# Clustered attention and two mixture layers on one core: direct transfers of the maxima's row, new places, and another form of the tail

## The chip, the cores and the metric

One Trainium2 chip, one of its cores. The metric is the device time of one launch in microseconds (us).

## The reference

Three layers in a row, all in float32:

```python
# attention: q, k, v of shape (4, 8, 768, 64), 16 centroids for each head
q_assign = argmax(normalised(q) @ normalised(c).T); k_assign = the same of k
scores = where(q_assign == k_assign, q @ k.T / 8, -1e9)
x = softmax(scores) @ v                       # to (3072, 512)
# first mixture layer: w_in (512, 2048), w_out (2048, 512)
h = x @ w_in; y = (h * cos(h)) @ w_out
# soft mixture: phi (512, 32), 8 experts of 4 slots, w1 (8, 512, 1024), w2 (8, 1024, 512)
logits = y @ phi
d = softmax over tokens; c = softmax over the 32 slots
slot_input = d.T @ y
slot_out[e] = relu(slot_input[e] @ w1[e]) @ w2[e]
out = c @ slot_out                            # (3072, 512)
```

## The kernel before, in words

**Attention.** The 32 heads are worked on in 16 pairs. Each pair has 12 units `u` (two halves of the queries, six blocks of 128 keys), and each unit has two scores, one for each head. `score` (L394) makes two matmuls, one with 97 rows (L399) and one with 128 (L400), from a stack tile `st` in SBUF that holds the split q and k, the cluster codes and, in partition 96, the negated row maxima. ScalarE takes the exponent (L403), `av` (L405) multiplies with `v` on TensorE two units later, and GpSimd adds up the denominators (L417, L420). The maxima come from `smax` (L354): 24 small score matmuls a pair (L364), each followed by a VectorE reduction (L366). They rotate through three PSUM banks. `smax_fin` (L368) merges 12 of them, and `smax_row` (L376) transposes the result on TensorE (L379), lets VectorE write `mrow` (L381), and defers two transfers: `mrow` to a DRAM tile `mds`, and `mds` to partition 96 of `st`.

Everything around the scores is put at numbered places by hand: a pair has 48 of them, four for each unit, and `POS` (L521) holds the places of the steps for a pair in the steady state, `FIRST` (L533) those for the first two pairs. For pair j, the preparation (`place_p`, L560: transposes "T", clusters "c", "m", code rows "rows", loading of the next pair "ld") runs two pairs ahead and the maxima ("sm", "fin") one pair ahead. The last "sm" of the first half of the queries and its "fin" have to be through by place 48, where the pair's first score stands. The conversion of the weights from 64-bit words ("cv", `conv_do` L455, eight steps, mostly VectorE's) handles two blocks a pair; its input comes through `conv_load` (L448) into one buffer, `w64`, and the weights' products with phi stand at "wp". "vm" has the places of the mean of v (`prep_vm`, GpSimd; `prep_vm2`, TensorE) and of `sumq` (L427), the sums of the denominators.

All transfers are issued by SP, in the order of the program. `defer(n, ...)` (L162) puts a transfer off by n places, and `tick` (L165), called at each place, issues what is due. A transfer that has to wait for its data holds up all that follow it on SP.

**First mixture layer.** 96 chunks `c` (token tile and quarter of the hidden width; the last two tiles are taken together). `hchunk` (L131) makes 12 matmuls, `post1`, `post2` the cosine, `gtr`, `gev`, `logit` the transposed product with the weights and phi, and `soft1` to `soft5` a running softmax of the group of tokens that is done. `xload` (L94) fetches a tile's numerators `xn` and reciprocals `rc`. In the last chunks the freed buffers take the experts' weights: 16 pieces of 2 MB (`load_piece`, `load_part`, `load_halves`, L740 to L754).

**Tail.** From L989 on: the last softmax, `apz`, `acct`, `si`, `sit` (the slots' input), `expert_in` (pieces 0 to 7), `expert_tr`, `expert_out` (L1140, pieces 8 to 15, 32 output columns of the array for each of four experts, so four column positions), and then for each half of the output width `regroup` (L1151) and twelve calls of `final` (L1161), which multiply the combination weights with the slots' output and write it out. Between them the combination weights `ck` are split into a high and a low part, twice each (`ct_dve`, L904), transposed to `ctk` (`ct_pe`, L910: 24 transposes in four groups) and evicted by ScalarE (`ct_ev`, L918). `final` then needs one fp32r matmul over 128 rows per token tile (L1168), evicted by ScalarE (L1172) or VectorE (L1174).

Of the kernel before, what the change touches and what calls it, by code (L numbers as in the profile page):

```python
# [19 lines left out]
P = 128  # L20
# [6 lines left out]
def clustered_attention_then_soft_moe(  # L27
# [60 lines left out]
    mds = {(i, c): dram.tile([6, P], F32, name=f"mds{i}_{c}") for i in range(NPAIR) for c in range(2)}  # L88
# [5 lines left out]
    def xload(t):  # L94
        b, tt = divmod(t, KT)
        c = slice(tt * P, (tt + 1) * P)
        mx = R["mx"]
        xn = mx.tile([P, DT, P], F32, tag="xn", name=f"xn{t}", bufs=1)
        rc = mx.tile([P, DT, P], F32, tag="rc", name=f"rc{t}", bufs=1)
# [50 lines left out]
    with ExitStack() as a:  # L150
# [225 lines left out]
        def smax_row(i, qc):  # L376
# [141 lines left out]
        def at4(g, q, f, *args):  # L518
# [14 lines left out]
        FIRST = {  # L533
            "eqt": 7,
            "mask": 8,
            "rows": [9, 12, 12, 10],
            "cv": [3, 6, 8, 11, 15],
            "ld": 9,
            "wp": [21, 26, 36],
            "sm0": [2, 2, 5, 5, 6, 7, 8, 12, 15],  # L540
            "sm1": [13, 15, 16, 21, 22, 24, 24, 25, 26, 26, 28, 29, 17, 29, 31, 33, 34, 38, 40, 41, 42, 42, 44, 45],
            "fin0": [15, 19],
            "fin1": [33, 35],
        }

        def place_conv(n, g):
# [3 lines left out]
            if n + 1 < len(conv):  # L550
                at(g + pos[5] // 4 + 1, 0, conv_load, n + 1)
# [69 lines left out]
        def m_open():  # L621
            pp_stack.close()
            R["mx"] = mx_stack.enter_context(tc.tile_pool(name="mx", bufs=2, side="right"))
# [124 lines left out]

    def load_halves(n, w):
        for e in range(2):  # L750
            load_part(n, 2 + e, w[:, e])
# [4 lines left out]
    with ExitStack() as m:  # L756
# [299 lines left out]
        for h in range(2):  # L1056
# [6 lines left out]
            if h == 0:  # L1063
                ct_pe(1)
# [159 lines left out]
```

## Time and profile before

| what | value |
|---|---|
| time, median of 3 runs | 959.75 us (957.63 to 960.16) |
| time of the profiled execution | 960.29 us |
| its span, first to last instruction | 958.4 us |
| mean granted TensorE clock | 0.989 |
| TensorE busy | 904.9 us, 94% |
| VectorE busy | 716.2 us, 75% |
| ScalarE busy | 674.5 us, 70% |
| GpSimd busy | 459.3 us, 48% |
| attention, first to last score | about 32 to 503 us |
| first mixture layer | about 504 to 890 us |
| tail | about 890 to 958 us |

PE is TensorE's matmuls, PEld its weight loads, DVE VectorE, ACT ScalarE, POOL GpSimd, SP the queue that issues the transfers. A wait names the engine and line that sat idle, then what ended it. In a windows row the granted clock (1.00 is 2.4 GHz), the DMA engines' busy share and the GB/s that they moved stand at the end. A matmul's end is modelled, so a matmul may count as busy while it waits to drain. An fp32 matmul shows as two instructions.

### The profile page before, as it was taken

What the parts mean: (1) busy time and instruction counts of PE and PEld (TensorE: products, weight loads), DVE (VectorE), ACT (ScalarE), POOL (GpSimd) and SP (SyncE); (2) the same over time, 40 slices, a digit from 0 to 9 for tenths busy, and PEclk for the clock granted to TensorE, in tenths of its full rate; (3) what the DMA queues carried; (4) which work ended last, traced back from release to release, by engine and by line L of the source; (5) the groups of instructions that cost most, each with busy time, mean ns of one, the idle gap of its engine ahead of it and who ended that gap; (6) DMA issues with size and microseconds to landing.
All of it is one profiled execution on the core that took longest, in us unless ns stands there. A gap on an engine that the chain in (4) does not pass through costs nothing.

```text
span 958.4 us, 16925 instructions
## 1 busy us (share of the span) xinstructions
PE 904.9 (94%) x5994; PEld 622.8 (65%) x5994; DVE 716.2 (75%) x1459; ACT 674.5 (70%) x1420; POOL 459.3 (48%) x342
## 2 busy tenths in 40 slices
PE   5798999999999999999999999999999999999995
PEld 3465666666666666656656777777777777677543
DVE  6778888988888888879786777777777777775402
ACT  4657888777887778867664677767776777676423
POOL 3437877788777878776862222222222222220000
PEclk9889999999999999999999999999999999999998
DMA  8966667776668766676231043304331111117899
GB/s 173 211 149 157 162 175 196 192 197 155 166 176 213 191 172 166 174 186 166 89 95 54 24 132 117 125 25 132 119 123 36 33 37 31 45 26 295 333 360 326
DMA packets 132515, 142.18 MB, mean 148 GB/s; under 512 B 58408, under 2 KB 105808, under 8 KB 132432
## 3 DMA queue, kind: packets, MB, share of 16 engines
q1 hardware_dynamic: 132432, 141.11, 53.2%
q8 instruction: 47, 0.77, 0.3%
q14 instruction: 36, 0.29, 0.1%
HBM read 86.27 MB, written 17.06 MB: 108 GB/s over the span
## 4 chain that ended last, share of the span: by engine, by line
PE 68%; DVE 11%; ACT 9%; DMA 7%; issue 2%; SPq 2%; POOL 0%; ACTq 0%; POOLq 0%
PE h L138 21%; PE o L412 12%; PE sm L364 6%; PE s L399 6%; PE s L400 5%; PE gt L784 3%; DVE mc L366 3%; DMA mds<-mrow 3%; PE lp L810 2%; PE accp L893 2%; DVE qlo L275 2%; ACT L772 2%; DMA st<-mds 2%; PE he L1101 1%; ACT L848 1%
## 5 line engine op out<-in xcount | busy, mean ns | idle before, releaser
L138 PE MATMUL h<-wc,xhi 128*128 128x512 f32 x768 | 249.6, 406 | 6.7 <-DVE gg L777 6.5
L420 POOL TENSOR_TENSOR ps<-ps,a 128x768 f32<-128x768 f32 x120 | 235.3, 1961 | 37.9 <-ACT a L403 18.2
L366 DVE TENSOR_REDUCE mc<-sm 128x1 f32<-128x384 f32 x384 | 199.1, 547 | 30.3 <-PE sm L364 27.9
L403 ACT ACTIVATE a<-s 128x384 f32<-128x384 f32 x384 | 175.8, 491 | 26.2 <-PE s L400 20.4
L138 PEld LDWEIGHTS h<-wc,xhi 128*128 128x128 f32 x768 | 137.3, 189 | 56.9 <-DVE kk L147 15.9
L138 PE MATMUL h<-wc,xlo 128*128 128x512 f32 x384 | 151.7, 395 | 0.0
L399 PE MATMUL s<-st 97*128 97x384 f32 x384 | 141.8, 369 | 7.3 <-DMA st<-mds 6.9
L412 PE MATMUL o<-a,vt 128*64 128x384 f32 x768 | 147.7, 506 | 0.0
L364 PE MATMUL sm<-st 96*128 96x384 f32 x384 | 135.8, 385 | 10.1 <-DVE mc L366 6.1
L400 PE MATMUL s<-st 128*128 128x384 f32 x384 | 130.5, 340 | 0.0
L364 PEld LDWEIGHTS sm<-st 96*128 96x128 f32 x384 | 72.4, 194 | 50.4 <-DVE mc L366 17.5
L777 DVE SCALAR_TENSOR_TENSOR gg<-kk,h 128x512 f32<-128x512 f32 x96 | 66.0, 687 | 50.6 <-ACT kk L774 47.8
L772 ACT ACTIVATE kk<-kk 128x512 f32<-128x512 f32 x96 | 60.6, 631 | 42.0 <-DVE kk L147 41.7
L399 PEld LDWEIGHTS s<-st 97*128 97x128 f32 x384 | 73.1, 190 | 23.1 <-issue 11.1
L412 PEld LDWEIGHTS o<-a,vt 128*64 128x64 f32 x768 | 47.2, 137 | 57.6 <-issue 57.3
L109 POOL TENSOR_TENSOR xn<-xn,rc 128x512 f32<-128x512 f32 x24 | 31.3, 1304 | 109.0 <-DMA rc<-recs 109.0
L138 PEld LDWEIGHTS h<-wc,xlo 128*128 128x128 f32 x384 | 72.2, 188 | 17.0
L400 PEld LDWEIGHTS s<-st 128*128 128x128 f32 x384 | 73.4, 191 | 0.0
L417 POOL TENSOR_TENSOR ps<-a,a 128x768 f32<-128x768 f32 x30 | 54.8, 1827 | 37.5 <-ACT a L403 33.7
L113 POOL TENSOR_TENSOR xn<-xn,rc 128x512 f32<-128x512 f32 x24 | 32.0, 1332 | 84.0 <-DVE rc L111 78.9
L121 POOL TENSOR_TENSOR xlo<-xn,xhi 128x512 fp32r<-128x512 f32 x24 | 36.5, 1522 | 67.5 <-DVE xhi L120 66.0
L147 DVE SCALAR_TENSOR_TENSOR kk<-kk,h 128x512 f32<-128x512 f32 x96 | 66.0, 688 | 3.3
(218 smaller groups left out, 1530.0 us busy)
## 6 DMA issues: line engine op xcount, KB each, us to landing
w<-in_moe_w_dram SPq DMA_DIRECT2D x8, 2048.0 KB
wh<-in_moe_w_dram SPq DMA_DIRECT2D x26, 512.0 KB
st<-qhi SPq DMA_DIRECT2D x32, 384.0 KB
st<-khi SPq DMA_DIRECT2D x64, 192.0 KB
w<-in_moe_w_out_dram SPq DMA_DIRECT2D x16, 512.0 KB
w<-in_moe_w_in_dram SPq DMA_DIRECT2D x16, 512.0 KB
qt<-in_q_dram SPq DMA_DIRECT2D x32, 192.0 KB
kt<-in_k_dram SPq DMA_DIRECT2D x32, 192.0 KB
```

Source lines behind the costliest of these rows:

```text
L138: PE.matmul(h, lhsT=x[:, d, :], rhs=wc[f][:, w, d, :], start=(n == 0), stop=(n == 3 * DT - 1))
L147: DVE.scalar_tensor_tensor(out=a, in0=a, scalar=-TWO_PI, in1=h, op0=ALU.mult, op1=ALU.add)
L364: PE.matmul(m[:, 0:QW], lhsT=st[0:96, Q1 + h, qt * P:(qt + 1) * P], rhs=st[0:96, K1 + h, half * QW:(half + 1) * QW], start=True, stop=True)
L366: DVE.tensor_reduce(out=s["mc"][:, col:col + 1], in_=m[:, 0:QW], op=ALU.max, axis=AX.X)
L399: PE.matmul(x[:, 0:QW], lhsT=st[0:97, K1 + h, ks], rhs=st[0:97, Q1 + h, qs], start=True, stop=False)
L400: PE.matmul(x[:, 0:QW], lhsT=st[:, K2 + h, ks], rhs=st[:, Q2 + h, qs], start=False, stop=True)
L403: ACT.activation(out=T[i][u][:, h, :], in_=x[:, 0:QW], func=AF.Exp, scale=scale)
L412: PE.matmul(s["o"][64 * h:64 * h + 64, 0:QW], lhsT=s["v"][:, h, kt, :], rhs=t[:, h, :], start=(kt == 0), stop=(kt == KT - 1))
L417: (DVE if i == NPAIR - 1 else POOL).tensor_tensor(out=ps, in0=s[u - 1], in1=t, op=ALU.add)
L420: (DVE if i == NPAIR - 1 else POOL).tensor_tensor(out=ps, in0=ps, in1=t, op=ALU.add)
L772: ACT.activation(out=r, in_=r, func=AF.Sin, scale=0.5)
L777: DVE.scalar_tensor_tensor(out=R["g", t][:, f * 512:(f + 1) * 512], in0=r, scalar=0.5, in1=h, op0=ALU.subtract, op1=ALU.mult)
```

## The change

1. `smax_row` no longer goes through DRAM: two transfers, one for each head, go from `mrow` in SBUF straight to `st`, both at the place where the write to DRAM stood. The tiles `mds` are gone.
2. All places in `POS` and `FIRST` are new. `conv_load` gets places of its own ("cl") and `w64` a second buffer.
3. `xn` and `rc` become one tile in a pool of its own, which lasts beyond the layer; when the last `xload` is through, its memory takes the part of piece 8 called `w8b`, at chunk 90. The memory that `w8b` had takes three more parts (`w9b`), and the remaining 23 parts follow in order.
4. For the second to last group of tokens `soft3b` and `soft3` come one chunk earlier.
5. Tail: `ck` is transposed as it is, four token tiles to one transpose (six in all, in two groups), with no split. `ctk` then holds four token tiles in the partition ranges 0, 32, 64, 96, and `final` makes four fp32 matmuls over 32 rows, one in each row position and each to a bank of its own, in four rounds of 1, 2, 2 and 1 such sets. `regroup` loses VectorE's subtraction. `expert_out` of pieces 8 to 11 is split by output half, and the second half comes later.

```diff
-        xn = mx.tile([P, DT, P], F32, tag="xn", name=f"xn{t}", bufs=1)
-        rc = mx.tile([P, DT, P], F32, tag="rc", name=f"rc{t}", bufs=1)
+        xr = R["mxa"].tile([P, 2, DT, P], F32, tag="xr", name=f"xr{t}", bufs=1)
+        xn, rc = xr[:, 0], xr[:, 1]
...
-            defer(DL, out=mds[i, qc], in_=mrow.bitcast(F32))
-            defer(DL + 6, out=st[96:97, Q1:Q1 + 2, QW * qc:QW * qc + QW].bitcast(F32),
-                  in_=mds[i, qc].rearrange("(o h t) p -> o h (t p)", h=2, o=1))
+            for h in range(2):
+                defer(DL, out=st[96:97, Q1 + h, QW * qc:QW * qc + QW].bitcast(F32).rearrange("o (t p) -> o t p", p=P),
+                      in_=mrow[3 * h:3 * h + 3].bitcast(F32))
...
-            st = two.tile([P, 1024], I32, tag="w64", name=f"w64_{n}", bufs=1)
+            st = two.tile([P, 1024], I32, tag="w64", name=f"w64_{n}")
...
         POS = {
-            "T": [3, 7, 0, 1, 7, 12, 17, 23],
-            "c": [12, 16],
-            "m": [16, 20, 25, 28],
-            "rows": [42, 35, 42, 36],
-            "ld": 16,
-            "cv": [[4, 4, 4, 8, 9, 12, 16, 17], [28, 29, 30, 35, 37, 42, 42, 45]],
-            "wp": [23, 34, 40],
-            "sm": [0, 5, 6, 7, 10, 10, 15, 17, 18, 26, 26, 27, 20, 21, 21, 32, 34, 36, 36, 40, 41, 43, 45, 46],
-            "fin": [1, 4, 30, 35],
-            "vm": [6, 28, 19],
+            "T": [3, 8, 0, 3, 9, 12, 16, 28],
+            "c": [11, 15],
+            "m": [19, 20, 26, 28],
+            "rows": [35, 35, 38, 43],
+            "ld": 8,
+            "cv": [[3, 5, 5, 10, 11, 14, 15, 23], [29, 29, 29, 36, 39, 42, 43, 45]],
+            "wp": [23, 29, 41],
+            "sm": [0, 6, 10, 14, 17, 21, 22, 25, 26, 26, 28, 34, 1, 10, 13, 24, 33, 34, 36, 37, 38, 40, 44, 44],
+            "fin": [3, 6, 34, 36],
+            "vm": [24, 30, 11],
+            "cl": [1, 41],
         }
...
-                at(g + pos[5] // 4 + 1, 0, conv_load, n + 1)
+                at4(g, POS["cl"][n % 2], conv_load, n + 1)
...
+            if at_last.get(c - 6) == [NT - GRP - 1]:
+                soft3b(at_last[c - 6])
+                soft3(at_last[c - 6])
+            elif at_last.get(c - 7) == [NT - GRP - 1]:
+                soft4(at_last[c - 7])
...
+            if c == NC_ - 6:
+                w8 = R["mxa"].tile([P, 1024], F32, tag="xr", name="w8b", bufs=1)
+                load_part(8, 2, w8)
...
-        w8 = wx.tile([P, 1024], F32, name="w8b")
-        load_part(8, 2, w8)
-        cbuf = wx.tile([P, 3840], F32R, name="cbuf")
+        w9b = wx.tile([P, 3, 1024], F32, name="w9b")
+        ctk = wx.tile([P, NT // 4, P], F32, name="ctk")
+        for x in range(3):
+            load_part(9 + (2 + x) // 4, (2 + x) % 4, w9b[:, x])
...
+        def ct_pe(x):
+            a, n = ((0, 4), (4, 2))[x]
+            g = psum.tile([P, 512], F32, tag=("m0", "m3")[x], name=f"ctk{x}")
+            for y in range(n):
+                PE.transpose(g[:, y * P:(y + 1) * P], ck[:, 4 * (a + y):4 * (a + y) + 4, :].rearrange("p t s -> p (t s)"), ident)
+            R["ct", x] = a, n, g
...
         def regroup(hf):
-            sp = spare.rearrange("p (a b) -> p a b", a=3)
             sos = hs[:, 256 * hf:256 * hf + 256]
             ACT.activation(out=sos, in_=so[hf], func=AF.Copy)
-            g = mbank(f"sor{hf}")[:, 0:256]
+            if hf == 0:
+                expert_out(9, hfs=(1,))
+            g = psum.tile([P, 512], F32, tag="s", name=f"sor{hf}", bufs=3)[:, 0:256]
             PE.matmul(g, lhsT=gflat, rhs=sos, start=True, stop=True)
-            st = stk[hf] = sp[:, 1 + hf]
+            st = stk[hf] = hs[:, 512 + 256 * hf:768 + 256 * hf]
             ACT.activation(out=st, in_=g, func=AF.Copy)
-            DVE.tensor_tensor(out=st[64:128], in0=g[64:128], in1=st[64:128], op=ALU.subtract)
...
+            g = [psum.tile([P, 512], F32, tag=f"m{q}", name=f"fo{hf}_{x}_{q}") for q in range(4)]
+            for y in range(n):
+                for q in range(4):
+                    PE.matmul(g[q][:, 256 * y:256 * y + 256], lhsT=ctk[32 * q:32 * q + 32, a + y, :],
+                              rhs=stk[hf][32 * q:32 * q + 32, :], start=True, stop=True)
...
         for n in range(8, 12):
-            expert_out(n)
+            expert_out(n, hfs=(0,))
         expert_tr(1)
+        expert_out(8, hfs=(1,))
         expert_out(12)
         expert_out(13)
         regroup(0)
-        for x in range(12):
-            if x % 3 == 0:
-                expert_out(14, [x // 3])
-            final(0, x // 3, x % 3)
+        for x in range(4):
+            expert_out(14, [x])
+            final(0, x)
+            if x < 2:
+                expert_out(10 + x, hfs=(1,))
         expert_out(15)
         regroup(1)
-        for x in range(12):
-            final(1, x // 3, x % 3)
+        for x in range(4):
+            final(1, x)
```

## Rows read from the trace of the kernel before

**Rows 1.** The page, part 1: busy time, share, instructions of each engine.

```profile
PE 904.9 (94%) x5994; PEld 622.8 (65%) x5994; DVE 716.2 (75%) x1459; ACT 674.5 (70%) x1420; POOL 459.3 (48%) x342
```

**Rows 2.** Busy time by stretch, in the attention: 38 us and 6 us.

```profile
core 0: us, PE busy (x) PEld busy (x) DVE busy (x) ACT busy (x) POOL busy (x), PEclk, DMA share, GB/s
300.00:338.00 38.00, 36.52 (x226) 23.75 (x224) 32.03 (x63) 31.95 (x71) 28.59 (x19) 1.00 0.73 184
426.00:432.00 6.00, 4.68 (x20) 2.23 (x20) 1.97 (x5) 2.43 (x7) 5.73 (x5) 0.72 0.31 95
```

**Rows 3.** TensorE's waits, 48 to 490 us: total, times, longest.

```profile
PE s L399 <- DMA st<-mds: 6.9, 7, 1.8
...
PE sm L364 <- DVE mc L366: 4.6, 8, 0.8
...
PEld s L399 <- DMA st<-mds: 9.9, 12, 2.1
```

**Rows 4.** Timeline of TensorE: start, duration, instruction, [idle before].

```profile
334.44 1.51 PE L412 MATMUL o<-a,vt 128*64 128x384 f32 x8
...
338.94 0.45 PE L399 MATMUL s<-st 97*128 97x384 f32 x1 [0.98 <-DMA st<-mds]
...
427.32 0.45 PE L399 MATMUL s<-st 97*128 97x384 f32 x1 [1.81 <-DMA st<-mds]
...
428.70 2.83 PE L412 MATMUL o<-a,vt 128*64 128x384 f32 x8
```

**Rows 5.** Timeline of SP's queue: the row's two transfers.

```profile
333.22 0.30 SPq L170 DMA_DIRECT2D mds<-mrow  x1
...
337.05 0.64 SPq L170 DMA_DIRECT2D st<-mds  x1
```

**Rows 6.** Waits of VectorE (DVE), 48 to 490 us.

```profile
DVE t L466 <- DMA w<-in_moe_w_out_dram: 28.3, 14, 3.7
```

**Rows 7.** VectorE by line, 100 to 450 us: busy, mean ns, idle.

```profile
L366 DVE TENSOR_REDUCE mc<-sm 128x1 f32<-128x384 f32 x285 | 148.3, 547 | 15.4 <-PE sm L364 13.4
...
L275 DVE TENSOR_TENSOR klo<-kT,khi 128x768 fp32r<-128x768 f32 x12 | 15.2, 1269 | 0.0
...
L466 DVE TENSOR_SCALAR t<-w 128x512 int32<-128x512 int32 x24 | 16.5, 689 | 26.6 <-DMA w<-in_moe_w_out_dram 26.6
```

**Rows 8.** Timeline of TensorE in the second to last group.

```profile
881.64 1.06 PE L893 MATMUL accp<-gg,dts 128*32 128x512 f32 x8 [0.55 <-ACT dts L883]
```

**Rows 9.** Busy time by stretch, in the tail.

```profile
890.00:895.00 5.00, 4.21 (x40) 2.73 (x39) 4.06 (x11) 2.77 (x7) 0.00 (x0) 1.00 1.02 401
895.00:900.00 5.00, 4.71 (x74) 3.02 (x78) 2.84 (x11) 3.07 (x11) 0.00 (x0) 1.00 0.62 237
900.00:905.00 5.00, 5.00 (x66) 2.47 (x58) 0.92 (x2) 1.06 (x3) 0.00 (x0) 1.00 0.66 255
950.00:955.00 5.00, 0.00 (x0) 0.00 (x0) 0.00 (x0) 0.00 (x0) 0.00 (x0) 0.55 1.03 344
```

**Rows 10.** The chain that ended last, 880 to 960 us: start, duration, what.

```profile
897.59 0.66 PE ctk L915 x6
...
902.62 0.69 PE ctk L915 x6
...
917.87 0.81 PE ctk L915 x6
...
944.28 0.44 DVE cbuf L1159
```

**Rows 11.** Timeline of the tail, all engines.

```profile
934.81 0.62 PE L1148 MATMUL so<-wh,htb 128*32 128x256 f32 x2 [0.88 <-DMA wh<-in_moe_w_dram]
...
940.70 1.93 PE L1148 MATMUL so<-wh,htb 128*32 128x256 f32 x32
...
944.77 3.96 PE L1168 MATMUL fo<-cbuf 128*128 128x256 f32 x24 [0.94 <-DVE cbuf L1159]
...
945.31 4.08 ACT L1172 ACTIVATE ob<-fo 128x512 f32<-128x512 f32 x8 [1.05 <-PE fo L1168]
```

More of the change, by code (lines that the diff above doesn't have):

```diff
@@ L622, in m_open @@
             pp_stack.close()
+            R["mxa"] = ctx.enter_context(tc.tile_pool(name="mxa", bufs=1, side="right"))
             R["mx"] = mx_stack.enter_context(tc.tile_pool(name="mx", bufs=2, side="right"))
@@ L1086, in clustered_attention_then_soft_moe, with load_next @@
         sit_half(0)
-        ct_pe(2)
+        ct_pe(1)
     if True:
-        for n in (9, 10):
-            load_halves(n, wk.tile([P, 4, 1024], F32, tag="wk", name=f"wh{n}"))
+        parts = [divmod(41 + x, 4) for x in range(23)]
+        def load_next(pool, tag):
+            w = pool.tile([P, 4, 1024], F32, tag=tag, name=f"wh{len(parts)}")
+            for x in range(min(4, len(parts))):
+                load_part(*parts.pop(0), w[:, x])
+        load_next(wk, "wk")
+        load_next(wk, "wk")
         ht, HE = {}, {}
@@ L1104, in expert_in @@
                     sit_half(1)
[L1105 to L1106 removed]
+                    ct_ev(1)
                 if n < 5:
[L1108 to L1109 removed]
+                    load_next(*((wk, "wk") if n < 4 else (wbig, "wbig")))
             HE[gi] = he
@@ L1146, in expert_out @@
             for hf, f, o in steps:
+                if hf not in hfs:
+                    continue
                 for j in range(4):
@@ L1158, in regroup @@
             ACT.activation(out=st, in_=g, func=AF.Copy)
-            DVE.tensor_tensor(out=st[64:128], in0=g[64:128], in1=st[64:128], op=ALU.subtract)
-        def final(hf, b, z3):
-            x, y = divmod(b, 2)
-            if y == 0 and z3 == 0:
-                pool, tag = obp[hf, x]
-                ob[hf] = pool.tile([P, 16, 256], F32, tag=tag, name=f"ob{hf}_{x}")
-            g = mbank(f"fo{hf}_{b}_{z3}")
-            for w in range(2):
-                PE.matmul(g[:, w * 256:(w + 1) * 256], lhsT=ctk[:, b * KT + 2 * z3 + w, :], rhs=stk[hf], start=True, stop=True)
-            o = ob[hf][:, 6 * y + 2 * z3:6 * y + 2 * z3 + 2, :]
-            gv = g.rearrange("p (a b) -> p a b", a=2)
-            if z3 % 2 == 0:
-                ACT.activation(out=o, in_=gv, func=AF.Copy)
-            else:
-                DVE.tensor_copy(o, gv)
-            first = hf == 1 and b == 0
-            t0 = 2 * z3 if first else 0
-            if first or z3 == 2:
-                SP.dma_start(out=out[b * S:(b + 1) * S, 256 * hf:256 * hf + 256].rearrange("(p t) d -> p t d", p=P)[:, t0:2 * z3 + 2],
-                             in_=ob[hf][:, 6 * y + t0:6 * y + 2 * z3 + 2, :])
+        ROUNDS = [(0, 1), (1, 2), (3, 2), (5, 1)]
@@ new lines, in final @@
+        def final(hf, x):
+            a, n = ROUNDS[x]
+            if x % 2 == 0:
+                pool, tag = obp[hf, x // 2]
+                ob[hf, x // 2] = pool.tile([P, 16, 256], F32, tag=tag, name=f"ob{hf}_{x // 2}")
+            o = ob[hf, x // 2][:, 0:12, :].rearrange("p (g r) d -> p g r d", r=4)
+            g = [psum.tile([P, 512], F32, tag=f"m{q}", name=f"fo{hf}_{x}_{q}") for q in range(4)]
[3 more added lines that the diff above has]
+                              rhs=stk[hf][32 * q:32 * q + 32, :], start=True, stop=True)
+            y = a % 3
+            for q in range(4):
+                ov, gv = o[:, y:y + n, q, :], g[q][:, 0:256 * n].rearrange("p (a b) -> p a b", a=n)
+                if q % 2 == 0:
+                    ACT.activation(out=ov, in_=gv, func=AF.Copy)
+                else:
+                    DVE.tensor_copy(ov, gv)
+            t0, t1 = 4 * a, 4 * (a + n)
+            if x == 2:
+                t1 = 18
+            if x == 3:
+                t0 = 18
+            while t0 < t1:
+                b = t0 // KT
+                e = min(t1, KT * (b + 1))
+                SP.dma_start(out=out[b * S:(b + 1) * S, 256 * hf:256 * hf + 256].rearrange("(p t) d -> p t d", p=P)[:, t0 - b * KT:e - b * KT],
+                             in_=ob[hf, x // 2][:, t0 % 12:t0 % 12 + e - t0, :])
+                t0 = e
```

72 lines of the change are left out of this document (18 added, 54 removed).

## The prediction

> **What bounds the kernel now.** I read the page first: TensorE is busy 94% of the span [rows 1]. That figure only says that its matmuls follow each other closely, so the question is where it waits. The busy time by stretch comes next: in the attention (one pair of heads after another from about 32 us to 503 us) TensorE stands still for 1.5 us of every 38, while VectorE is 84% busy, ScalarE 84% and GpSimd 75% [rows 2]. TensorE is first there, but three engines stand close behind it, and a gap closed on TensorE can open again behind one of them. Then the table of waits, cut to the attention: TensorE's largest single wait is for the maxima's row (`st<-mds`), 6.9 us in 7 waits as the matmuls show it and 9.9 us in 12 as the weight loads show it [rows 3]. The second figure is nearer to the delay, since a matmul that was issued late still counts as busy while its predecessor drains. The timeline shows one of these waits from close by: the wait stands in front of the first score of a new pair. The one at 427 us, 1.81 us long, is followed by a stretch at the lower of TensorE's two clock levels, 1.2 GHz (the slice has 0.72 of full speed in the mean), in which eight `o` matmuls take 2.83 us in place of 1.51 [rows 2, 4]. Two such first scores, at 338.94 and 427.32, lie three pairs apart: 29.5 us a pair, so one of the 48 places of a pair is 0.61 us long.
>
> In the tail the picture is another. From about 905 us the DMA engines are full to the end (share 1.03 still at 950 to 955, with no engine computing), and the only hole in front of that is 895 to 905, at shares of 0.62 and 0.66 [rows 9]. So the end is set by bytes, and what can be won is what moves into that hole, if compute keeps up.
>
> **The maxima's row.** Today SP writes 3 KB to DRAM, waits until it has landed, and only then issues the read back: at 333.22 and 337.05, 3.8 us for the first leg [rows 5]; behind that wait stands everything else of SP's queue. The new form issues two SBUF-to-SBUF transfers of 1.5 KB where the write stood, with no wait between them; the number of issues stays two. No row has such a transfer. From above I bound it by the DRAM leg just named, 3.8 us; from below by nothing at all. The row is now produced at place 36 and its transfers stand at 39, nine places or 5.5 us before the pair begins at 48, so even the upper bound fits with 1.7 us to spare. I take 9.0 of the 9.9 us as won; the ends are 6.9 and 9.9, and the larger is nearer because it counts the late issue itself. The slow stretch after the stall at 427 should go with its cause: six microseconds at 0.72 are 1.7 us of clock, and I take 1.5 (ends 0 and 1.7).
>
> **The weights' conversion.** VectorE waits 28.3 us in 14 waits for the staged weights [rows 6], about 2 us at the start of each pair, because the one buffer is freed late. Two buffers, and a load asked for at place 41 instead of 44, take that wait away. VectorE is not the bound there, and TensorE stands in the row's wait during most of it, so by itself I cost it at nothing. It matters for the next point: with the row's stall gone, this wait would have been the next to show.
>
> **The new places.** What replaces the waits is VectorE's queue. The last reduction of the first half's maxima moves from place 27 to 34, its `smax_fin` from 30 to 34 and the transposition on TensorE from 35 to 36. From place 28 to that transposition VectorE gets `klo` (1.27 us), two conversion steps (1.38), four reductions (2.19) [rows 7] and a very short reduction: 4.8 us of work in eight places, 4.9 us. Before, from `klo` at place 23, it had 4.3 us in twelve places, 7.3 us. The reserve falls from 3.0 us to 0.1, and any backlog at place 28 is then waited for by TensorE. The least it costs is nothing; a gain is not excluded either, since 4.6 us of waits for `mc` exist [rows 3] and may fall. The most is three reductions queued, as the maxima rotate through three banks: 1.65 us a pair, 23 us over the 14 pairs placed so. I take 0.2 us a pair, 3 us, as VectorE's own reserve grows by the 2 us that it no longer waits. `sumq` at 11 instead of 19 follows GpSimd's last additions, and `prep_vm` at 24 comes in an engine with a quarter of its time free [rows 2]; both at nothing, and their cover is that free time. The places of the first two pairs I cost at nothing too; no row prices them, and the nearest, the 4.6 us for `mc` in the pairs behind, bounds them either way.
>
> **Second to last group.** Moving its `soft3b` one chunk ahead takes away TensorE's wait of 0.55 us for `dts` [rows 8]: 0.5 us. The merged `xn`/`rc` buffer changes no order on SP, which waits for `xn` first already.
>
> **The tail.** Transfers: `w8b` is asked for some 25 us earlier, where the DMA engines have room, and in its old place stand three parts of 512 KB, 1.57 MB. At the 401 GB/s of 890 to 895 that is 3.9 us of traffic, and the hole offers 5 x 0.38 + 5 x 0.34 = 3.6 us [rows 9]. Compute: three groups of transpositions leave the chain (0.66, 0.69 and 0.81 us) and about 0.3 of them stays; VectorE's subtraction of 0.44 goes [rows 10]; the 0.88 us that TensorE waits for the last part of piece 14 goes with the earlier loads [rows 11]. That is 3.2 us. The final products become fp32 of 32 rows: 48 instructions a half. No row has row positions. Side by side like the four column positions of `so` (32 in 1.93 us, 0.24 us for each four), a half takes 2.9 us; one after another, 11.5; now `fo` spans 3.96 us, at ScalarE's pace, which evicts for 4.08 us [rows 11]. I take the lower price, as the column positions are the nearest row. The Trainium skill's page TensorEngine Tiling (Array Packing), PSUM Bottleneck, warns that tiling speeds up TensorE "but not PSUM evacuation"; the trace agrees with the 4.08 us of `ob`, and by it the last half gains nothing, by the matmuls alone 1 us. My sum gives it nothing, because four banks per round must be emptied before the next round: roughly 2 us longer on the last half, hidden under its own writing, since its 3.1 MB at the 344 GB/s of 950 to 955 take 9 us after the first eviction [rows 9]. With 3.6 us offered by the transfers and 3.2 by compute, I take 2.5 us (ends: 3.6 won, 8.5 lost when the positions run one after another).
>
> **The sum.** The profiled execution took 960.29 us (span 958.39 and 1.9 around it): 960.29 - 9.0 - 1.5 - 0.5 - 2.5 + 3.0 = 949.8. It is 0.5 us over the median of the runs, so I predict 949.5.
>
> **Rivals.** *VectorE becomes late at place 36.* For it: the reserve of 0.1 us, and VectorE's 84%. Against it: the 2 us that it stops waiting. It cancels the 13.5 us of gains at 0.96 us a pair; with the full queue of 1.65 us the time is 960.3 - 13.5 + 23.1 = 969.9, slower than before. *The stall keeps its size under another name*, as the row lands late after all, or another input of the first score or maximum is the next to be late: for it speaks that four engines are over 75% busy; then only tail and second to last group pay, 957. *The four row positions do not run side by side*: each half 8.6 us longer, both on the path, less what the 9 us of writing hide; the tail is then at +8.5 (17.2 less 8.7) instead of -2.5, 960.8. Against it stand the column positions. The Trainium skill's TensorE: Matmul & The Clock Gate, Part 3, reports 3.07 times the speed for four row positions, which no run here shows; by an estimate from that figure and the 11.5 us a half takes 3.7 us. *More is won*: VectorE without its 28 us of waits also answers the other maxima sooner, and in place of the 3 us of new waits the 4.6 us for `mc` go [rows 3]: 942.
>
> **How the numbers follow.** Forecast (944 to 954) 0.50; more won (937 to 944) 0.15; stall under another name (954 to 960) 0.17; row positions in turn (955 to 962) 0.08; VectorE late (over 962) 0.10. A measurement here can tell 0.3%, 2.9 us. Faster by more: the first two, half of the third, a quarter of the fourth, 0.75; within: 0.13; slower: 0.12. A range of 940 to 960 leaves out the late VectorE and the lower half of "more won", 0.17 or so.
>
> **What the new profile would show.** Right: no wait for `st` by the row, no waits of VectorE for the staged weights, a pair near 28.8 us, no slow clock in the attention but at its start, DMA share near 1 throughout 895 to 905, the `fo` matmuls of four positions starting together, last eviction and end both some 2.5 us earlier against the start of the tail. Wrong: waits of TensorE for `m` before the transposition or for `mc` after place 28, the pair still 29.4 us long, or `fo` sets of 0.9 us and more.

## The result, and the profile after

The changed kernel takes 933.09 us (median of four runs, 932.76 to 934.25) against 959.95 us (957.63 to 961.21) for the kernel before on the same chip: a ratio of 0.9716, 95% interval 0.9686 to 0.9745. It is 27 us faster; I had predicted 949.5 us, ten faster, and the time lies below the range of 940 to 960. The profiled execution has a span of 931.1 us, the one before 958.4.

The page, part 1, answers to [rows 1]: the share of TensorE rises by two points, and VectorE is busy for 24 us less, though no step of the change removes that work: three groups of instructions, the same in number, take 28 us less (last section).

```profile
PE 892.3 (96%) x6024; PEld 621.6 (67%) x6024; DVE 692.5 (74%) x1457; ACT 671.4 (72%) x1414; POOL 462.1 (50%) x342
```

Busy time by stretch, the two stretches of [rows 2]:

```profile
300.00:338.00 38.00, 38.00 (x241) 25.51 (x238) 31.95 (x60) 31.21 (x70) 32.80 (x25) 1.00 0.78 197
426.00:432.00 6.00, 6.00 (x36) 3.85 (x34) 5.93 (x13) 5.82 (x13) 3.06 (x3) 1.00 0.50 174
```

TensorE is busy for all of the 38 us (36.52 before), with 241 matmul instructions in place of 226, and the stretch of slow clock at 426 is gone. The table of waits, 48 to 490 us, turns round what [rows 3, 6] showed:

```profile
DVE mc L364 <- PE sm L362: 60.1, 98, 2.5
...
PEld s L397 <- issue: 25.1, 52, 0.6
...
PEld sm L362 <- DVE t L474: 8.4, 14, 0.6
```

No row wait is left, and VectorE, which was late before, now waits 60 us for TensorE. What TensorE's weight loads still wait for is mostly of one length, 0.6 us, whatever name stands beside it (8.4 us in 14 waits here).

**Where the 27 us went.** The first score of each pair (the 97-row matmul) cuts both attentions into 16 stretches. In us, from the timelines:

```
                       before   after
start of pair 1          32.4    31.9
pair 1, pair 2     41.9, 29.9   36.8, 29.0   -6.0
pairs 3 to 14           353.2   332.1       -21.1   (29.4 and 27.7 a pair)
pairs 15, 16       24.9, 20.9   24.8, 21.1   +0.2
last score to end       455.2   455.3        +0.1
```

All of it lies in the attention. (The first pair scatters: 36.4 to 40.3 us in the nine profiles of kernels with the new list for the first two pairs, 41.9 to 45.5 in the six with the old one.) From the last score to the end, where I had 3.0 us (the second to last group and the tail), these two profiles show no change. In the changed kernel eleven of the twelve pairs from the third on last 27.70 us to the last digit, and TensorE's matmuls show no idle time in them: a pair has become a fixed length, as far as the profile shows that of TensorE's own instructions.

**The tail after.** TensorE's timeline and the DMA share, to be read against [rows 9, 11]:

```profile
904.91 0.62 PE L1138 MATMUL so<-wh,htb 128*32 128x256 f32 x2 [0.89 <-DMA wh<-in_moe_w_dram]
905.46 0.71 PE L1162 MATMUL fo<-gl,ctk 32*128 32x256 f32 x8
...
907.53 1.15 PE L1162 MATMUL fo<-gl,ctk 32*128 32x256 f32 x16
908.61 1.50 PE L1138 MATMUL so<-wh,htb 128*32 128x256 f32 x24
...
913.22 1.93 PE L1138 MATMUL so<-wh,htb 128*32 128x256 f32 x32
916.83 0.71 PE L1162 MATMUL fo<-gl,ctk 32*128 32x256 f32 x8 [0.47 <-ACT gl L1149]
917.99 1.54 PE L1162 MATMUL fo<-gl,ctk 32*128 32x256 f32 x16 [0.45 <-ACT ob L1168]
919.81 1.91 PE L1162 MATMUL fo<-gl,ctk 32*128 32x256 f32 x16 [0.27 <-ACT ob L1168]
921.99 1.95 PE L1162 MATMUL fo<-gl,ctk 32*128 32x256 f32 x8 [0.27 <-ACT ob L1168]
```

```profile
895.00:900.00 5.00, 5.00 (x84) 3.18 (x80) 0.00 (x0) 1.09 (x2) 0.00 (x0) 1.00 1.10 349
900.00:905.00 5.00, 3.98 (x49) 1.67 (x42) 0.00 (x0) 0.77 (x2) 0.00 (x0) 1.00 1.10 348
905.00:910.00 5.00, 5.00 (x74) 2.44 (x74) 2.01 (x4) 1.74 (x4) 0.00 (x0) 1.00 1.08 348
910.00:915.00 5.00, 4.92 (x68) 2.83 (x64) 2.17 (x5) 1.85 (x4) 0.00 (x0) 1.00 0.89 309
915.00:920.00 5.00, 3.30 (x32) 1.94 (x29) 1.51 (x4) 2.27 (x6) 0.00 (x0) 1.00 0.84 284
920.00:925.00 5.00, 3.67 (x24) 2.50 (x23) 2.67 (x5) 2.09 (x5) 0.00 (x0) 0.72 0.88 298
```

The weights do land earlier: the last part of piece 14 is waited for at 904.91, 46.8 us after the last `hchunk` matmul began (858.09), before 49.5 (934.81 less 885.29). But piece 15's products start 55.1 us after it, before 55.4: what was won at the gate is spent behind it, where TensorE now takes 8.3 us (904.91 to 913.22) and took 5.9. In it stand 32 instructions of the halves put off (piece 15's 32 take 1.93 us), and the rounds are longer. And the DMA engines, full to the end before, are now at 0.84 to 0.89 from 910 to 925: the bytes alone no longer set the pace there. The last half's products reach from 916.83 to 923.94, 7.1 us against 3.96 [rows 11], because each round of four banks waits until ScalarE has emptied them (`<-ACT ob`). The four row positions themselves do run side by side: 16 instructions in 1.15 us, 0.29 for each four.

### The profile page after: what moved, and what is told of

Its sections match the earlier page's. It is cut to its first block, busy times and chain, and to the rows that moved or that the text cites. A ratio compares the mean times of both kernels' runs of the same rounds, so it can differ in the third digit from the quotient of the medians.

```text
span 931.1 us, 17027 instructions
## 1 busy us (share of the span) xinstructions
PE 892.3 (96%) x6024; PEld 621.6 (67%) x6024; DVE 692.5 (74%) x1457; ACT 671.4 (72%) x1414; POOL 462.1 (50%) x342
## 4 chain that ended last, share of the span: by engine, by line
PE 74%; ACT 8%; DVE 7%; issue 4%; DMA 3%; SPq 2%; POOL 1%; POOLq 0%; ACTq 0%
PE h L136 16%; PE o L410 15%; PE s L397 9%; PE sm L362 8%; PE s L398 7%; PE gt L777 2%; PE lp L803 2%; SPq L741 2%; ACT L765 2%; DVE gg L770 2%; PE accp L886 2%; ACT L841 2%; PE cl L288 1%; PE tpq L247 1%; ACT kk L765 1%
## 5 line engine op out<-in xcount | busy, mean ns | idle before, releaser
L364 DVE TENSOR_REDUCE mc<-sm 128x1 f32<-128x384 f32 x384 | 203.9, 553 | 69.3 <-PE sm L362 66.5
L418 POOL TENSOR_TENSOR ps<-ps,a 128x768 f32<-128x768 f32 x120 | 236.2, 1968 | 19.0 <-ACT a L401 14.3
L401 ACT ACTIVATE a<-s 128x384 f32<-128x384 f32 x384 | 180.1, 493 | 29.6 <-PE s L398 26.5
L136 PEld LDWEIGHTS h<-wc,xhi 128*128 128x128 f32 x768 | 137.3, 189 | 57.4 <-DVE kk L145 15.9
L410 PE MATMUL o<-a,vt 128*64 128x384 f32 x768 | 145.1, 499 | 0.0
L397 PE MATMUL s<-st 97*128 97x384 f32 x384 | 143.7, 374 | 0.0
L362 PE MATMUL sm<-st 96*128 96x384 f32 x384 | 130.8, 374 | 2.8 <-DVE st L335 1.6
L362 PEld LDWEIGHTS sm<-st 96*128 96x128 f32 x384 | 71.6, 193 | 29.3 <-DVE t L474 8.4
L765 ACT ACTIVATE kk<-kk 128x512 f32<-128x512 f32 x96 | 60.6, 631 | 42.2 <-DVE kk L145 41.9
L107 POOL TENSOR_TENSOR xr<-xr 128x512 f32<-128x512 f32 x24 | 31.1, 1295 | 110.1 <-DMA xr<-recs 107.4
L398 PEld LDWEIGHTS s<-st 128*128 128x128 f32 x384 | 73.1, 190 | 0.0
L111 POOL TENSOR_TENSOR xr<-xr 128x512 f32<-128x512 f32 x24 | 31.4, 1307 | 82.9 <-DVE xr L109 79.2
L119 POOL TENSOR_TENSOR xlo<-xr,xhi 128x512 fp32r<-128x512 f32 x24 | 36.5, 1523 | 68.1 <-DVE xhi L118 68.1
```

The costliest lines, as they stand in the source:

```text
L136: PE.matmul(h, lhsT=x[:, d, :], rhs=wc[f][:, w, d, :], start=(n == 0), stop=(n == 3 * DT - 1))
L362: PE.matmul(m[:, 0:QW], lhsT=st[0:96, Q1 + h, qt * P:(qt + 1) * P], rhs=st[0:96, K1 + h, half * QW:(half + 1) * QW], start=True, stop=True)
L364: DVE.tensor_reduce(out=s["mc"][:, col:col + 1], in_=m[:, 0:QW], op=ALU.max, axis=AX.X)
L397: PE.matmul(x[:, 0:QW], lhsT=st[0:97, K1 + h, ks], rhs=st[0:97, Q1 + h, qs], start=True, stop=False)
L398: PE.matmul(x[:, 0:QW], lhsT=st[:, K2 + h, ks], rhs=st[:, Q2 + h, qs], start=False, stop=True)
L401: ACT.activation(out=T[i][u][:, h, :], in_=x[:, 0:QW], func=AF.Exp, scale=scale)
```

## Experiments: the row and the staged weights

Three theories stood behind the first four runs: that the row's stall and VectorE's late conversion trade against each other, so that one grows where only the other is mended; that the row's stall is a loss of its own, of the size that its name has in the table of waits; and that the order of the work is what pays. All three fell.

**Direct transfers alone**, in the kernel before:

```diff
-            defer(DL, out=mds[i, qc], in_=mrow.bitcast(F32))
-            defer(DL + 6, out=st[96:97, Q1:Q1 + 2, QW * qc:QW * qc + QW].bitcast(F32),
-                  in_=mds[i, qc].rearrange("(o h t) p -> o h (t p)", h=2, o=1))
+            for h in range(2):
+                defer(DL, out=st[96:97, Q1 + h, QW * qc:QW * qc + QW].bitcast(F32).rearrange("o (t p) -> o t p", p=P),
+                      in_=mrow[3 * h:3 * h + 3].bitcast(F32))
```

> The kernel before with the direct transfers of the row alone (old places, one staging buffer, old tail). The attention, first to last score, lasts 470.9 us before and 443.9 us after. Theory of exchange (the row's wait and VectorE's late queue cover for each other, so mending one lets the other grow): 3 to 7 us shorter, and waits of TensorE for mc grow. Rival of single sizes (each wait goes with its own size): 9 to 11 us shorter, about 950 in all. Rival of places (the order of the work is what pays): under 3 us shorter.

**The second buffer with its earlier loads alone**, in the kernel before:

```diff
-            st = two.tile([P, 1024], I32, tag="w64", name=f"w64_{n}", bufs=1)
+            st = two.tile([P, 1024], I32, tag="w64", name=f"w64_{n}")
...
-                at(g + pos[5] // 4 + 1, 0, conv_load, n + 1)
+                at4(g, POS["cl"][n % 2], conv_load, n + 1)
```

(with `"cl": [1, 41]` in `POS`.)

> The kernel before with the second staging buffer and its loads at places 1 and 41 alone. Exchange: the 28 us of VectorE's waits go, the attention gets 2 to 8 us shorter, and the wait for the row stays or grows above 9.9 us. Single sizes: no change in time, as VectorE's wait was costed at nothing. Places: under 3 us.

**Both of them, with the old places:**

> Direct transfers and second buffer together, old places. Exchange: more than e1 and e2 added, 13 to 20 us shorter. Single sizes: e1 plus nothing, 9 to 11 us. Places: at most 8 us, the remaining 19 or more needing the places.

**The new places without either of them** (the changed kernel with the row through DRAM, one buffer and the old rule for its load):

> The kernel after with the row through DRAM again and one staging buffer, loaded where the old rule puts it (places 16 and 44): new places and new tail alone. Exchange: both waits stay, so the attention is 0 to 10 us shorter than before, most of it in the first pair. Single sizes: some 5 us shorter (first pair). Places: 18 us shorter or more.

Measured, one run each, against 959.5 us of the kernel before on the same chip: direct transfers 943.64, second buffer 948.67, both 940.89, the new places without either 987.0. The direct transfers alone brought 15.9 us, more than any theory had and more than their wait has by name. The second buffer brought 10.8, again above all three. Both together brought 18.6, inside the 13 to 20 of the exchange, but far less than the two added (26.7), so mending one did not let the other grow in its place. And the new places alone are 27.5 us slower, where every theory had a gain. To see why, I sorted the idle time ahead of weight loads in pairs 3 to 14 by its length (without the loads of `o`, which have 0.2 us each among themselves in every kernel). The last three lines are the runs further down:

```
                          over 0.7 us   0.55 to 0.7    0.15 to 0.55   pairs 3 to 14
before                    13: 15.0 us    95: 57.5 us    57: 13.0 us    353.2 us
direct                     1:  0.9       96: 58.1       39:  8.2       334.8
buffer                     4:  4.9       96: 58.1       41:  8.4       338.9
direct + buffer            0             96: 58.1       36:  7.3       333.4
after (with new places)    0             84: 50.6       60: 11.9       332.1
places alone              25: 41.0       83: 50.0       71: 15.5       380.9
after, one buffer         11: 14.1       84: 50.6       60: 11.9       345.6
after, row through DRAM    9:  8.7       84: 50.6       68: 14.3       343.2
before, buffer, old load  11: 11.1      102: 61.6       61: 14.3       354.7
```

Three things are in it. The long waits, 15.0 us, go as a whole with either edit, give or take a few, so the two edits are substitutes: 18.5 and 14.3 us alone, 19.8 together. Some 5 us of short waits go with them. And the middle column is mostly no lateness at all: 8 waits of 0.60 us in each pair, in every kernel with the old places (a few late ones of that length come on top in the last line, and one is longer in the first). They stand where the tiling of TensorE's array changes, from `o`, `cl` or `sum` with 64 or 32 output columns to something else. The new places put `cl` and `sumq` next to one another, which takes away one of the eight (7 a pair, 84).

**The second buffer with the load where it was** tells apart what could link the two edits: a buffer that is freed late, or SP's queue.

```diff
-            st = two.tile([P, 1024], I32, tag="w64", name=f"w64_{n}", bufs=1)
+            st = two.tile([P, 1024], I32, tag="w64", name=f"w64_{n}")
```

> The kernel before with a second buffer for the staged weights and nothing else: the load keeps its place, behind the row's read back on SP's queue. Theory (VectorE is late because SP's queue holds the load while it waits for the row's first leg to land; the buffer alone changes nothing in that): VectorE's wait for the staged weights stays above 15 us, pairs 3 to 14 stay at 348 to 353 us, time 956 to 960. Rival (what delayed the load was the buffer, freed late by VectorE itself): the wait for the staged weights falls under 5 us and the time to 948 to 951, as with the second buffer and the earlier load together (948.7).

Measured: 961.96 us against 958.7 for the kernel before beside it (ratio 1.0032, 0.9999 to 1.0065): no gain, the theory's side, with the time and pairs 3 to 14 (354.7 us) a little above its ranges. VectorE's waits in this kernel, 97 to 456 us, and SP's queue:

```profile
DVE t L466 <- DMA w<-in_moe_w_out_dram: 28.1, 12, 3.7
```

```profile
336.45 0.28 SPq L170 DMA_DIRECT2D mds<-mrow  x1
340.21 0.65 SPq L170 DMA_DIRECT2D st<-mds  x1
340.91 0.39 SPq L452 DMA_DIRECT2D w<-in_moe_w_out_dram  x1
```

The load goes out right behind the row's read back, and the read back waits 3.8 us for the write to land. In the kernel before it is the same: the read back of [rows 5] at 337.05 is followed by the load, and VectorE's wait ends 3.5 us after that:

```profile
337.80 0.36 SPq L452 DMA_DIRECT2D w<-in_moe_w_out_dram  x1
```

```profile
341.30 0.69 DVE L466 TENSOR_SCALAR t<-w 128x512 int32<-128x512 int32 x1 [2.67 <-DMA w<-in_moe_w_out_dram]
```

With the load at 41 it stands between the two legs of the row (SP's queue, second buffer with the earlier loads):

```profile
329.09 0.28 SPq L170 DMA_DIRECT2D mds<-mrow  x1
329.42 0.36 SPq L452 DMA_DIRECT2D w<-in_moe_w_out_dram  x1
330.89 0.65 SPq L170 DMA_DIRECT2D st<-mds  x1
```

So the loop is this: SP waits for the row to land; the load behind it is late; VectorE waits 1.5 to 3.7 us for it at the head of its queue, with the maxima's reductions behind; the next row is made late; TensorE waits for that row. It can be cut at either end. With the direct row SP has no landing to wait for, and VectorE's wait falls from 26.6 us to 8.4 (97 to 456 us) with the load in its old place. With the earlier load VectorE is on time, and TensorE's wait for the row falls from 6.9 us in 7 to 1.2 in one, though the row still goes through DRAM. (The earlier load with one buffer was not run, so what the buffer adds to it stays open.)

## Experiments: the new places

**One buffer and the old load rule, in the changed kernel** (the second diff above, reversed):

> The changed kernel with one buffer for the staged weights and the old rule for their load; the direct row, the new places and the new tail stay. Theory (direct transfers and second buffer replace one another, since either alone brought 14 to 19 of the 21 us of pairs 3 to 14): the direct row is enough, VectorE waits for the staged weights again but TensorE hardly feels it; pairs 3 to 14 about 333 to 335 us (332.1 in the changed kernel), time 934 to 937. Rival (the new places have no reserve on VectorE, 0.1 us by my count, and need both): each conversion that starts late delays the maxima of the same pair, 0.5 to 1.5 us a pair, 940 to 952.

**The row through DRAM, in the changed kernel** (the first diff above, reversed):

> The changed kernel with the row through DRAM as before; the second buffer, its load at 1 and 41, the new places and the new tail stay. Theory (the new places need the direct row: the row is produced at 36, the write stands at 39, the read back at 45, and the first leg took 3.8 us, six places, so the read back lands after 48 and the first score of the pair waits): first scores wait 1 to 2.5 us in each of 14 pairs, time 950 to 970, waits of TensorE for the row 14 to 30 us, and little of the rest of what the kernel with both undone (987) lost. Rival (either of the two is enough also at the new places): 934 to 938.

Measured: 948.8 us (two runs) and 944.3 us (two runs), where the changed kernel has 933.1. At the old places the direct row did nearly without the second buffer (943.64 against 940.89); at the new ones each is worth 11 to 16 us. For the first of the two kernels the rival held. For the second both expectations missed: pairs 3 to 14 are longer by 0.9 us each, and not at their first scores, where I had waits of 1 to 2.5 us. The waits name the new chain (one buffer; TensorE's weight loads, then one stretch of ScalarE's timeline):

```profile
PEld sm L362 <- ACT vm L350: 14.1, 11, 1.9
```

```profile
322.94 0.66 ACT L468 ACTIVATE val<-w 128x512 f32<-128x512 f32 x1 [1.66 <-DMA w<-in_moe_w_in_dram]
323.88 0.16 ACT L350 ACTIVATE vm<-vm 128x1 f32<-128x1 f32 x1
```

One step of the conversion is ScalarE's. It waits 1.66 us for the staged weights, and behind it in ScalarE's queue stands the eviction of `vm`, moved to place 30 by the change, which frees the bank that the next maximum's matmul wants. So the late load now reaches TensorE through ScalarE. In the other kernel the row is late by itself:

```profile
PE s L398 <- DMA st<-mds: 6.1, 9, 1.0
```

Only one of these nine waits stands in front of the first score of a pair (0.29 us); the others stand in front of the first score of the second half of the queries. The row of the first half, whose production moved from 30 and 35 to 34 and 36, is nearly always in time, also through DRAM. The late one is produced at 3 and 6 (before at 1 and 4). SP's queue, and the score that waits:

```profile
248.89 2.20 SPq L177 DMA_DIRECT2D qt<-in_q_dram  x2
...
252.58 0.48 SPq L169 DMA_DIRECT2D mds<-mrow  x1
...
256.99 0.62 SPq L169 DMA_DIRECT2D st<-mds  x1
```

```profile
259.60 0.42 PE L398 MATMUL s<-st 97*128 97x384 f32 x1 [1.02 <-DMA st<-mds]
```

VectorE has the row ready at 249.2, but it goes out only at 252.58, behind the loads of the next pair's `q` and `k`, which the change moved from place 16 to 8 ("ld"). That this order is the cause I read from the queue; no run moved "ld" alone. With both edits undone the first scores of the pairs wait too, and the waits grow to what the places alone cost, 27 us over the kernel before:

```profile
PE s L398 <- DMA st<-mds: 27.4, 21, 2.3
...
PEld s L398 <- ACT kT L249: 23.5, 12, 2.5
```

**The old list for the first two pairs, in the changed kernel** (`FIRST` as before the change):

> The changed kernel with the old places for the first two pairs only. Theory (the new list for the first two pairs is worth what the kernels with old places lost there, 73.8 us for two pairs with both transfers mended, against 65.8): first two pairs 72 to 75 us, granted clock under 0.9 in the first 75 us, pairs 3 to 14 still 332 us, time 940 to 942. Rival (the first two pairs became shorter through the places of the pairs behind them or through the transfers): first two pairs about 66 us, time 933 to 935.

Measured: 938.38 us (two runs), first two pairs 45.4 and 28.4 us, pairs 3 to 14 332.1, granted clock 0.89 in the first 75 us (1.00 in the changed kernel). The theory held for the stages, though the time lies 1.6 us below its range and the first score was 1.9 us sooner here (30.05), so that the first two pairs end 6.1 us later than in the changed kernel. TensorE's timeline shows the place (this kernel, then the window around it):

```profile
36.26 0.88 PE L247 MATMUL tpk<-ident,kt 128*128 128x128 f32 x3 [4.89 <-DMA kt<-in_k_dram]
```

```profile
36.00:42.00 6.00, 5.75 (x22) 4.89 (x23) 2.74 (x5) 3.24 (x7) 1.81 (x1) 0.50 1.05 211
```

and the changed kernel at the same time:

```profile
33.55 0.34 PE L317 MATMUL eqt<-identb,eq 128*128 128x128 bf16 x3 [0.57 <-ACT a L401]
34.47 0.32 PE L324 MATMUL mt<-eqT,cum 128*128 128x384 bf16 x1 [0.58 <-ACT eqT L319]
35.08 0.44 PE L362 MATMUL sm<-st 96*128 96x384 f32 x1 [0.28 <-DVE mc L364]
36.14 0.52 PE L247 MATMUL tpk<-ident,kt 128*128 128x128 f32 x3 [0.61 <-DMA kt<-in_k_dram]
```

The `k` of a pair to come lands at about 36 us in both. With the old list TensorE stands in front of its transposition for 4.89 us, and then runs the next 6 us at 0.50, the lower clock level, where those transpositions take 0.88 us instead of 0.52. The new list has the mask's work (`eqt`, `mask` at 2) and more maxima in that gap, and the clock stays at 1.00. The kernel before, with the same old list, waits only 1.55 us for `k` there; its slow stretch comes later, behind a wait of 1.52 us for a maximum at 44.81:

```profile
48.00:51.00 3.00, 3.00 (x9) 1.51 (x11) 1.60 (x3) 0.49 (x1) 1.08 (x1) 0.50 1.05 248
```

## Experiments: the tail

**The halves not put off:** second halves of pieces 8 to 11 are multiplied before `expert_tr(1)`, as before the change.

```diff
         for n in range(8, 12):
-            expert_out(n, hfs=(0,))
+            expert_out(n)
         expert_tr(1)
-        expert_out(8, hfs=(1,))
```

(and the calls for pieces 9 to 11 in `regroup` and behind `final` go.)

> The changed kernel with the second halves of pieces 8 to 11 multiplied before the second group's transpositions, as before the change, with no halves put off. Theory (the halves put off stand behind the gate of piece 14 and lengthen TensorE's chain from there to the last piece): 0.9 us that TensorE waits at that gate is filled, the first writes start no later, the last piece's products start 1 to 2 us sooner against the end of the MoE layer, time 0.5 to 1.5 us shorter (931.5 to 932.5). Rival (TensorE is busy without a gap from 895 to 904, so the work only delays the first half's writes by what it saves later): 933 to 934.5, first half's first eviction 1 to 2 us later.

**Other banks for the last half's odd rounds:**

```diff
-            g = [psum.tile([P, 512], F32, tag=f"m{q}", name=f"fo{hf}_{x}_{q}") for q in range(4)]
+            if x % 2 and hf:
+                g = [psum.tile([P, 512], F32, tag="s" if q else "v", name=f"fo{hf}_{x}_{q}", bufs=3 if q else 1) for q in range(4)]
+            else:
+                g = [psum.tile([P, 512], F32, tag=f"m{q}", name=f"fo{hf}_{x}_{q}") for q in range(4)]
```

> The changed kernel with the odd rounds of the last half's final products in four PSUM banks that stand empty there, instead of the same four as the even rounds. Theory (the last half grew from 4.6 to 7.6 us because each round waits until its banks are emptied): the span from its first matmul to its last eviction falls to 5.5 to 6.2 us, and the end comes 1 to 1.5 us sooner (931.5 to 932). Rival (the end is set by the bytes that are still to be written, and an eviction that is sooner only waits for the queue): same 933, with 8 us instead of 6.7 between the last eviction and the end.

**Both:**

> Both edits of the tail together. Theory of the chain through TensorE: the two add, 1.5 to 3 us, 930 to 931.5, which beats both kernels. Rival (bytes set the end): 933 to 934.

Measured: 933.15 us (930.25 to 933.75), 929.5 (929.4 to 931.83) and 932.2 (931.37 to 934.01), four runs each. In the first run TensorE no longer waits for piece 14. Its layer ended later (last `hchunk` matmul at 859.99, in the changed kernel at 858.09), so I count from there: piece 15's products start 54.28 us behind it, after 55.13, and the first half's first eviction comes at 48.49, after 48.10. The rival's delay of 1 to 2 us did not come, and of the theory's 1 to 2 us there are 0.9; the eight profiles with the halves put off have 54.4 to 56.6, the two without 54.28. So the halves put off seem to cost a little, less than the times can show. The third lies between its theory and its rival. With other banks the waits between rounds are gone, TensorE's and ScalarE's timelines:

```profile
916.59 3.67 PE L1165 MATMUL fo<-gl,ctk 32*128 32x256 f32 x48 [0.47 <-ACT gl L1149]
```

```profile
918.18 2.62 ACT L1171 ACTIVATE ob<-fo 128x512 f32<-128x512 f32 x6 [0.20 <-PE fo L1165]
```

3.67 us in one piece in place of 7.1. What that is worth at the end I tested with both kernels on one chip:

> The changed kernel as it is, on the same chip as the next one. Either theory of the tail: 933, from the first part of the gate of piece 14 to the end 26.2 us.

> The changed kernel with the odd rounds of the last half's final products in other banks, beside the changed kernel. Theory (the banks cost time at the end): 2 to 4 us under the changed kernel, as the medians of the first runs have it (929.5 against 933.1). Rival (the end goes by the bytes still to be written): 0 to 1 us, as the two profiled executions have it from the gate to the end (25.5 against 26.2 us).

Measured: 933.3 us (931.37 to 934.27) and 932.05 (930.16 to 935.25), six runs each. The ranges overlap; the runs don't tell the two apart, and the 3.6 us between the first medians did not come again. The stage itself scatters less: from the last `hchunk` matmul to the end of the span the six profiles with the new tail and the shared banks took 72.1 to 74.6 us, 73.0 in the mean, the two with other banks 71.6 and 71.7, the one with the halves not put off 71.8, the one with both 71.2. So the banks are worth about 1.3 us, between the rival's 0 to 1 and my 2 to 4: most of the 3.4 us that compute gains goes into the queue of writes, as from the last eviction to the end it is now 8.8 us in place of 6.7. Which of these kernels is the fastest the runs cannot say.

## Why the prediction was wrong

- **The row's stall, -9.0, and the slow clock, -1.5.** The direction was right, and the wait is gone. The size failed: I read the loss from the wait's own name. The direct transfers alone bring 18.5 us in pairs 3 to 14, since SP's wait also held the load behind it. I wrote that "behind that wait stands everything else of SP's queue" and gave it no price. The question what is queued there, asked of the load, would have led to VectorE's 28.3 us.
- **The weights' conversion, at nothing.** This is the step that failed worst. I argued that VectorE is not the bound and that TensorE stands in the row's wait meanwhile. I also put VectorE's wait down to the one buffer, freed late; with two buffers and the old load it stays at 28.1 us, so it was the load's place behind the row's read back. The second buffer with its earlier loads is worth 14.3 us alone, as VectorE's lateness was a cause of the row's wait and not something beside it. As the edits are substitutes, the two terms together are 19.8, against the 10.5 that I gave them.
- **The new places, +3.0.** Wrong sign in the steady state: 332.1 against 333.4, a gain of 1.3, less than the 7.2 that one 0.60 us wait fewer in each pair would give, as the short waits grow by 4.6. They do leave less room: without the two edits the same places are 27 us over the kernel before, and with one of them the kernel is 11 to 16 us over the changed one. But the waits there are for the row and for ScalarE, and with the row through DRAM it is the second half's row that is late, so that VectorE's 0.1 us before place 36 is what ran out is not shown. My rival of the late VectorE did not come about: VectorE waits 60 us for TensorE's maxima.
- **The first two pairs, at nothing.** They gave 6.0 us, and with the old list put back they end 6.1 us later. "No row prices them" was wrong: the trace of the kernel before has waits of 1.5 us in the first pair and a stretch at the lower clock level.
- **Second to last group and tail, -3.0.** Measured +0.1 behind the last score in the two profiles; the group's 0.5 can't be seen in the 382 us of that layer, which scatter by 2 us between profiles. The transfers came 2.7 us sooner, close to the 2.5 to 3.6 that I had. But of the compute that I let go with them 2.4 us came back behind the gate (the 32 instructions put off and the longer rounds), and the 2 us that I gave the four banks as hidden were 3.1, of which the runs with other banks show about 1.3 as not hidden: the DMA engines were no longer full there. Over all profiles the tail is 73.0 us against 73.7 (five with the old tail, 73.1 to 74.4), 0.7 in place of 2.5.
- **The row positions** run side by side, as I took them: 2.9 us a half by my sum, 3.67 measured once the banks are out of the way. The Trainium skill's TensorEngine Tiling (Array Packing), PSUM Bottleneck, which I had set beside the 4.08 us of ScalarE, named what lengthens the last half here, the evacuation: within the 7.1 us the waits name it, and with other banks they are gone.

In the sum, against the profiled execution of 932.76 us: 949.8 - 6.0 (first two pairs) - 9.3 (the loop, 19.8 less 10.5) - 4.3 (the places, 1.3 and the 3.0) + 3.1 (tail and group) - 0.3 (start and last two pairs) = 933.0. This closes because both are stages of the same two profiles; of the single terms the first pair alone scatters by 3.9 us between profiles with the new list. (The recorded 949.5 is 0.2 more than 949.8 less the 0.5 that it names.)

## What to carry to other kernels

When one queue's wait stands in front of work for a second engine, and that engine makes what the first wait is for, the table of waits splits a single loss into names; price the loop by the length of a period against the sum of its bound engine's instructions, not by one name. Ask of each blocking wait on a transfer queue which load is issued behind it. And a tighter order is worth little by itself, but spends the reserve that other edits create: at the old places either edit was enough, at the new ones both are needed.

## What the runs showed of the hardware

When TensorE goes on from `o`, `cl` or `sum` (64 or 32 output columns, a moving operand of 384 columns) to another tiling, the next weight load stands idle for 0.60 to 0.63 us, 95 times in twelve pairs before and 84 after, under whatever releaser the trace names. I had taken such entries for waits. Not every change has this length: behind `wp`, with 32 output columns but a moving operand of 128, it is 0.20 us, and on the way into `o` 0.18 to 0.28 in the changed kernel. Its weight loads:

```profile
282.08 0.16 PEld L496 LDWEIGHTS wp<-wt,phis 128*32 128x32 f32 x8 [0.24 <-issue]
282.44 0.19 PEld L397 LDWEIGHTS s<-st 97*128 97x128 f32 x1 [0.20 <-issue]
...
284.44 0.20 PEld L410 LDWEIGHTS o<-a,vt 128*64 128x64 f32 x4 [0.25 <-issue]
...
285.88 0.19 PEld L362 LDWEIGHTS sm<-st 96*128 96x128 f32 x1 [0.60 <-DVE m L369]
```

What such an entry costs in time is not shown: the matmuls show no idle time there, and a pair with one of them fewer is 0.12 us shorter (27.70 against 27.82 at the old places). The Trainium skill's TensorEngine Tiling (Array Packing), Key Properties, says that a change of the tiling mode drains TensorE. The trace agrees in that these weight loads stand idle, with lengths that differ by what ran before.

The same VectorE instruction takes up to three times as long by its place: `eq` of 128x384 had 1.62 us before and 0.56 after, and in the mean of twelve pairs `qlo` had 1.90 and 1.25, `klo` 1.27 and 0.95. VectorE's timeline, before and then after:

```profile
263.23 1.62 DVE L312 TENSOR_TENSOR eq<-e,amx 128x384 bf16<-128x384 f32 x1
```

```profile
276.45 0.56 DVE L310 TENSOR_TENSOR eq<-e,amx 128x384 bf16<-128x384 f32 x1
```

What GpSimd did at those times, before and after:

```profile
260.11 8.92 POOL L420 TENSOR_TENSOR ps<-ps,a 128x768 f32<-128x768 f32 x4
```

```profile
276.05 0.46 POOL L342 TENSOR_TENSOR vs<-vt 128x128 f32<-128x128 f32 x1
276.58 2.35 POOL L344 TENSOR_TENSOR vs<-vs,vt 128x128 f32<-128x128 f32 x4
```

Before, `eq` falls into four additions of GpSimd that take 2.23 us each, where single ones elsewhere take 1.82 to 1.83: both engines are slower in that stretch. After, `eq` also falls into additions of GpSimd (`vs`) and keeps its 0.56 us; those four take 2.35 us, where in the kernel before they take 2.06 and 2.07. That the engines slow one another is my reading and was not tried by itself. The Trainium skill's SBUF — State Buffer, Who interferes with whom, says that a VectorE instruction with two inputs in SBUF contends with a GpSimd instruction that reads SBUF; the rows agree with that, as `eq` has two inputs; what it costs, and whom, differs between them. It did not set the time here: with the direct row, the second buffer and the old places `eq` still takes 1.45 us, and a pair is 27.8 us long.
